# Five VectorE operations instead of six per block of float64 weights, and the adds of the second token product moved from GpSimd to VectorE

## The chip, the cores and the metric

The kernel runs on one core of one Trainium2 chip. The metric is the device time of one execution in microseconds (us), smaller is better. A run of the kernel is given by the median of its executions. One execution was also recorded by the hardware profiler; its lines are called the profile or the trace here. The engines are PE (TensorE: matmuls), PEld (its weight loads), DVE (VectorE), ACT (ScalarE), POOL (GpSimd) and SP (which only starts transfers). Each engine works through its own queue in order.

## The reference: what is computed

Hashed attention (4 batches, 8 heads, 768 positions, head size 64) followed by one mixer layer. The weights come from `randn(...).astype(float32) * (1.0 / np.sqrt(n))`, which gives **float64** arrays; the kernel has to round them to float32 itself.

```python
mask = q_bucket[:, :, :, None] == k_bucket[:, :, None, :]
scores = np.where(mask, scale * q @ k.T, -1e9)
x = softmax(scores) @ v                    # (B, S, 512)
h = np.maximum(xt @ w_tok1, 0.0) @ w_tok2  # xt: x with tokens last
u = x + h.transpose(0, 2, 1)
return u + np.maximum(u @ w_ch1, 0.0) @ w_ch2
```

w_tok1 is 768x256, w_tok2 256x768, w_ch1 512x1536, w_ch2 1536x512.

## The kernel before, in words

Three stages follow each other, each with its own pools, and each with the order of every queue written out by hand.

**Attention** (`attention`, from L266) goes over 16 pairs of heads. Per pair PE makes scores in 12 chunks (L345), ACT takes the exponentials (L352), DVE adds the chunks up (L379 to L386), PE multiplies with the values (`weigh`, L397), and DVE and ACT make quotients (`Quotients`: L425 to L448). In each pair one step of a weight conversion is laid between: `weights.join()` after `newton()`, and `weights.turnover()` after `divide()`. Twelve blocks are converted in this stage (w_tok1, w_tok2, w_ch1).

**Tokens** (`tokens`, L600) goes over the 4 batches b. `mix1(b)` is the first token product (L641), followed on ACT by a relu (L648). `left_sums(b)` (L664 to L667, DVE) prepares the left operands of the second product. `mix2(b, m)`, for m = 0 and 1, is the second token product. For b = 0 it is computed directly (L690, L694). For b = 1 to 3 it is a form with seven products instead of eight: ACT copies partial results out of PSUM (L703, L706, L708, L710) to four parts p1, u, p7, p57 of a buffer `to`, and five adds (L713 to L717) finish them there. A transfer started by POOL (L681, `store`) then adds the buffer to XT in memory. Buffers come from three `places` in turn: `mix2(b, m)` uses number (2b + m + 1) mod 3, so that (3,1) uses the one that (2,0) used, and its first copy L703 must wait until the store of (2,0) has landed. The order is: mix1(1), left_sums(1), mix2(0,0), job, mix2(0,1), weight sums, mix1(2), left_sums(2), mix2(1,0), job, mix2(1,1), mix1(3), left_sums(3), mix2(2,0), job, mix2(2,1), mix2(3,0), `inputs` (L594, L595), mix2(3,1). Two more jobs lie in each mix1, behind its relus. The first job makes sums for w_ch1; the others are `slot`s of the conversion of w_ch2, 8 blocks.

**Channels** (`channels`, L754) does the two channel products in nested forms with seven products (all matmuls at L782) and stores the result.

**A conversion** (`Conversion`, L140) works on blocks of 128 x 768 weights. `fetch` loads the raw 64-bit words to SBUF with a transfer by SP (L168). `begin` shifts the high word left by 3 and puts its sign bit back (L179, L182: the result `big` is a float32 number cut off below). `join` makes the unit of the last place from it (L194), multiplies it with the low word (L198) and adds (L199). `end` takes the square of the high word on ACT (L211) and uses it to set numbers that are too small to zero (L212). A `slot` in the token stage ends the block before, fetches, and does begin and join of the next one, so that there is one slot more than blocks. In attention, join and end of a block come one pair after its begin.

What sets who waits for whom: with `bufs=3` (tokens) a raw buffer is free again when the last instruction that reads it is done, which in tokens is the square L211; in attention (`bufs=2`) it is L212.

Of the kernel before, what the change touches and what calls it, by code (L numbers as in the profile page):

```python
# [36 lines left out]
F32 = mybir.dt.float32  # L37
BF16 = mybir.dt.bfloat16
U32 = mybir.dt.uint32
I32 = mybir.dt.int32  # L40
I64 = mybir.dt.int64
ALU = mybir.AluOpType
ACT = mybir.ActivationFunctionType
# [5 lines left out]
def kernel(  # L49
# [13 lines left out]
    nc = tc.nc  # L63
    P = 128
    B, NP, _, _, S = qk.shape
    D = 64
    NB = proj.shape[1]
    DM = NP * P
# [5 lines left out]
    NHT = DCH // P  # L74
# [58 lines left out]

    NW = 768

    LEAST = float.fromhex("0x1.2p-15")
    double = w_tok1.dtype == I64
    NE = 2 if double else 1

    class Conversion:  # L140


        def __init__(self, pool, parts, bufs, apart=False):
            self.pool, self.bufs, self.apart = pool, bufs, apart
            self.todo = [
                (w, dst, rows, j, n)
                for w, dst, rows, blocks in parts
                for j in range(*blocks, rows)
                for n in range(0, dst.shape[2], NW // rows)
            ]  # L150
            self.fetched, self.begun, self.ready = [], None, None
            for _ in range(bufs - 1):
                self.fetch()
# [17 lines left out]
        def begin(self):  # L171
            if not self.fetched:
                return
            raw, to, rows = self.fetched.pop(0)
            hi = raw[:, :, 1]
            tmp = self.pool.tile([P, 2, NW], F32, name="tmp", tag="cvt", bufs=1)
            big = tmp[:, 0].bitcast(U32)

            nc.vector.tensor_scalar(  # L179
                big, hi, 3, 0x3FFFFFFF, op0=ALU.logical_shift_left, op1=ALU.bitwise_and,  # L180
            )
            nc.vector.scalar_tensor_tensor(  # L182
                big, hi, 0xC0000000, big, op0=ALU.bitwise_and, op1=ALU.bitwise_or,
            )
            self.begun = raw, tmp, to, rows

        def join(self):
            if not self.begun:
                return
            raw, tmp, to, rows = self.begun  # L190
            self.begun = None
            lo, hi = raw[:, :, 0], raw[:, :, 1].bitcast(F32)
            big, unit = tmp[:, 0], tmp[:, 1]
            nc.vector.tensor_scalar(  # L194
                unit.bitcast(U32), big.bitcast(U32), 0xFF800000, None, op0=ALU.bitwise_and,
            )

            nc.vector.scalar_tensor_tensor(unit, lo, 2.0**-52, unit, op0=ALU.mult, op1=ALU.mult)  # L198
            nc.vector.tensor_tensor(big, big, unit, op=ALU.add)  # L199
            self.ready = hi, big, to, rows  # L200

        def end(self):

            if not self.ready:
                return
            size, big, to, rows = self.ready
            self.ready = None
            hi = size
            if self.apart:
                size = self.pool.tile([P, NW], F32, name="size", tag="size", bufs=1)  # L210
            nc.scalar.activation(size, hi, ACT.Square)  # L211
            nc.vector.scalar_tensor_tensor(  # L212
                to, size.rearrange("p (t n) -> p t n", t=rows), LEAST * LEAST,
                big.rearrange("p (t n) -> p t n", t=rows), op0=ALU.is_ge, op1=ALU.mult,
            )

        def turnover(self):

            self.end()
            self.fetch()  # L220
            self.begin()

        def slot(self):

            self.end()
            self.fetch()
            self.begin()
            self.join()

    pairs = [(b, hp) for b in range(B) for hp in range(NP)]  # L230

# [34 lines left out]
    def attention(pool, psum, W1, W2, x0):  # L266
# [191 lines left out]
        for _ in range(12):  # L458
# [5 lines left out]
            bufs=2,  # L464
# [4 lines left out]
        for n in range(len(pairs)):  # L469
            halves = [Half(n, half) for half in range(2)]  # L470
            if n:
                load_v(n + 1)
            for now in halves:
                now.scores()
                if n == now.half == 0:
                    hashes(1)
                now.add()
                if now.half == 0:
                    now.add_last()
            if before:  # L480
                before.sums()
            if 0 < n < len(pairs) - 1:
                hashes(n + 1)
            halves[1].add_last()
            if n == 0:
                load_v(1)
            load_qk(n + 2)
            add_values(n)
            if before:
                before.newton()  # L490
            weights.join()
            halves[0].weigh()
            if n + 1 == len(pairs):
                before.divide()
                before = Quotients(halves)
                before.sums()
                before.newton()
                weights.turnover()
                halves[1].weigh()
                break  # L500
            if before:
                before.divide()
            weights.turnover()
            halves[1].weigh()
            if n and n % 2 == 0:
                bounce(pool.tile([P, 2 * S], F32, name="stage", tag="stage", bufs=1), n - 2)
            if n == 2 * NP:
                fetch(0, x0)
            before = Quotients(halves)
# [90 lines left out]
    def tokens(pool, psum, W1, W2, x0, weights, jobs, T, places):  # L600
# [68 lines left out]
        def mix2(b, m):  # L669

            r1, new = R1[b]
            a00, a01, s1, a11 = (
                r1[:, k, P * (2 * m + i) : P * (2 * m + i) + P] for i in range(2) for k in range(2)
            )
            new = new[:, :, P * m : P * m + P]
            ps = [bank("t2")[:, :HALF] for _ in range(4)]
            to = places[(2 * b + m + 1) % 3].rearrange("p (i n t) -> p i n t", i=2, n=2)
            p1, u, p7, p57 = (to[:, i, n] for i in range(2) for n in range(2))

            def store():  # L680
                nc.gpsimd.dma_start(  # L681
                    out=XT[:, 2 * m : 2 * m + 2, S * b : S * b + S], in_=to.rearrange("p i n t -> p i (n t)"),
                    accum_op=ALU.add,
                )

            if not b:
                for n in range(4):
                    for k in range(NJ):
                        at = P * (2 * m + n // 2)
                        nc.tensor.matmul(  # L690
                            ps[n], r1[:, k, at : at + P], W2[:, k, HALF * (n % 2) : HALF * (n % 2) + HALF],
                            start=(k == 0), stop=(k == NJ - 1),
                        )
                    nc.scalar.copy(to[:, n // 2, n % 2], ps[n])  # L694
                return store()

            def product(at, left, right, start=True):
                nc.tensor.matmul(  # L698
                    ps[at], left, right, start=start, stop=True, skip_group_check=True,
                )  # L700

            product(0, a00, b00)
            nc.scalar.copy(p1, ps[0])  # L703
            product(1, a01, b10)
            product(2, s1, sums[:, 0])
            nc.scalar.copy(p57, ps[2])  # L706
            product(3, new[:, 1], b01)
            nc.scalar.copy(p7, ps[3])  # L708
            product(0, new[:, 0], sums[:, 1], False)
            nc.scalar.copy(u, ps[0])  # L710
            product(2, new[:, 2], b11, False)
            product(3, a11, sums[:, 2], False)
            nc.vector.tensor_tensor(p1, ps[1], p1, op=ALU.add)  # L713
            (nc.gpsimd if b + 1 < B else nc.vector).tensor_tensor(p57, p7, p57, op=ALU.add)  # L714
            nc.vector.tensor_tensor(p57, p57, u, op=ALU.add)  # L715
            nc.vector.tensor_tensor(p7, ps[3], u, op=ALU.add)
            nc.vector.tensor_tensor(u, ps[2], u, op=ALU.add)  # L717
            store()
# [652 lines left out]
    def attention_and_tokens(W1, W2, x0):  # L1371
# [11 lines left out]
        second["tile"] = second_tile  # L1383

        def weights(pool):
            return Conversion(pool, [(w_ch2, WC2, 3, (0, NHT))], bufs=3, apart=True)

        def jobs(conversion):
            early, late = weight_sums(
                WC1, SW1, slice(0, NCB // 2), slice(NCB // 2, NCB), slice(0, DCH // 2), slice(DCH // 2, DCH),  # L1390
            )
            return [
                lambda: (early(), late()),
                *[conversion.slot] * (NHT * DM // NW + 1),
            ]

        SW2 = second["SW2"].rearrange("p i k c -> p i (k c)")
# [3 lines left out]
    def careful_attention_and_tokens(W1, W2, x0):  # L1401
        def weights(pool, psum):
            conversion = Conversion(pool, [(w_tok1, W1, 3, (0, NR)), (w_tok2, W2, 1, (0, NJ))], bufs=3)
            while conversion.fetched or conversion.ready:
                conversion.slot()

        def turned(pool, psum):
            turn(0, x0, lambda: psum.tile([P, 2, 512], F32, name="trp", tag="tr", bufs=2))
# [58 lines left out]
```

## Time and profile before

| | |
|---|---|
| median of 6 runs | 806.91 us (805.8 to 809.95) |
| the profiled execution | 806.37 us |
| its span, first to last instruction | 804.6 us, 10632 instructions |
| mean granted TensorE clock | 0.998 |
| busy: DVE, ACT, POOL | 672.1, 441.3, 57.1 us |
| attention, tokens, channels (PE from, to) | 14.5 to 315.9, 315.9 to 397.1, 397.4 to 798.2 us |

Lines of the profile have a start in us from the beginning of the span, a duration, the engine, the line of the kernel, the operation, and its output and inputs by name. `t` is a PSUM bank, `tmp` and `size` are scratch of the conversion, `second` in the token stage is a place of `mix2`, or the converted w_ch2. `x4` counts instructions that were merged into one line; each float32 matmul of the code is two PE instructions (mix1 has 12 matmuls and 24 instructions). In brackets is how long the engine had been idle before, and the instruction that ended the wait.

### The profile page before, as it was taken

To read this page: it belongs to the slowest core of one execution; us is meant where nothing else is said; L and a number is where in the kernel's file an instruction comes from. 1 tells how busy PE (TensorE), PEld (TensorE's weight loads), DVE (VectorE), ACT (ScalarE), POOL (GpSimd) and SP (SyncE) were. 2 spreads that over 40 slices of the span, in tenths; PEclk is the share of its full clock that TensorE was granted. 3 is DMA by queue.
4 is the path that set the end of the run, shared out by engine and by line. 5 is a ranking of instruction groups with operands and counts; after the bars stand their busy time and mean duration, and the time that the engine had idled before them with its cause. 6 is when DMAs were issued, how large, how long until landed. Compare 5 with 4: busy or idle time off the path is not lost.

```text
span 804.6 us, 10632 instructions
## 1 busy us (share of the span) xinstructions
PE 795.0 (99%) x3889; PEld 471.3 (59%) x3889; DVE 672.1 (84%) x884; ACT 441.3 (55%) x707; POOL 57.1 (7%) x80
## 2 busy tenths in 40 slices
PE   9999999999999999999999999999999999999996
PEld 5444444444444444455444458876666886666885
DVE  4789999999998677989867879888769897778986
ACT  5688888888888886243323221237773335775111
POOL 1000000000000000022221010011100012000000
PEclk9999999999999999999999999999999999999999
DMA  4435353537352424886646895499754578630454
GB/s 162 158 121 159 121 160 122 160 121 238 128 163 108 142 62 157 235 249 172 154 79 205 287 368 198 158 284 260 249 141 137 216 216 199 209 114 1 156 184 114
DMA packets 90701, 138.09 MB, mean 172 GB/s; under 512 B 29640, under 2 KB 63376, under 8 KB 88336
## 3 DMA queue, kind: packets, MB, share of 16 engines
q1 hardware_dynamic: 82480, 112.47, 42.1%
q0 software_dynamic: 7456, 24.12, 13.3%
q8 instruction: 33, 0.54, 0.3%
q10 hardware_dynamic: 704, 0.74, 0.3%
q14 instruction: 28, 0.23, 0.1%
HBM read 97.21 MB, written 33.16 MB: 162 GB/s over the span
## 4 chain that ended last, share of the span: by engine, by line
PE 95%; DVE 2%; issue 1%; POOL 0%; ACT 0%; DVEq 0%; POOLq 0%
PE b L782 49%; PE sc L345 20%; PE acc L397 16%; PE t L641 4%; PE sums L421 2%; PE t L690 1%; PE hp L306 1%; PE t L698 1%; PE hw L324 1%; PE idle L459 0%; DVE second L713 0%; DVE tmp L179 0%; DVE second L715 0%; POOL second L714 0%; DVE second L212 0%
## 5 line engine op out<-in xcount | busy, mean ns | idle before, releaser
L352 ACT ACTIVATE e<-sc 128x768 f32<-128x768 f32 x192 | 154.0, 810 | 13.0 <-PE sc L345 12.6
L345 PE MATMUL sc<-qk 64*128 64x384 f32 x768 | 156.7, 487 | 0.0
L782 PE MATMUL b<-R,second 128*128 128x256 f32 (+1 forms) x612 | 150.9, 404 | 0.0
L782 PEld LDWEIGHTS b<-R,second 128*128 128x128 f32 x612 | 116.3, 190 | 31.6 <-issue 17.2
L788 ACT COPY c<-b 128x512 f32<-128x512 f32 (+1 forms) x78 | 37.4, 488 | 169.7 <-PE b L782 155.4
L397 PE MATMUL acc<-e,vn 128*64 128x384 f32 x768 | 127.6, 488 | 0.0
L383 DVE TENSOR_TENSOR esd<-esd,e 128x768 f32<-128x768 f32 x96 | 92.0, 958 | 10.0
L397 PEld LDWEIGHTS acc<-e,vn 128*64 128x64 f32 x768 | 53.6, 137 | 73.1 <-issue 71.8
L345 PEld LDWEIGHTS sc<-qk 64*128 64x128 f32 x768 | 67.5, 187 | 49.5 <-issue 46.6
L782 PE MATMUL b<-XT,WC 128*128 128x256 f32 (+1 forms) x264 | 82.6, 457 | 0.2 <-DVE second L713 0.2
L782 PEld LDWEIGHTS b<-XT,WC 128*128 128x128 f32 x264 | 50.1, 190 | 30.2 <-issue 24.9
L345 PE MATMUL sc<-bits 64*128 64x384 bf16 x384 | 62.9, 323 | 0.2 <-DVE bits L328 0.2
L379 DVE SCALAR_TENSOR_TENSOR esd<-e 128x768 f32<-128x768 f32 x32 | 30.3, 948 | 17.6 <-ACT e L352 17.6
L641 PE MATMUL t<-x,W 128*128 128x512 f32 x96 | 41.8, 593 | 0.0
L442 ACT COPY rec<-rec 32x384 f32<-32x384 f32 x64 | 32.6, 509 | 10.1 <-DVE rec L436 9.5
L681 POOL DMA_DIRECT2D XT<-second x8 | 9.9, 1236 | 382.9 <-DVE tmp L198 338.5
L782 PE MATMUL b<-XT,SW 128*128 128x256 f32 (+1 forms) x120 | 34.6, 422 | 0.0
L345 PEld LDWEIGHTS <-bits 64*128 64x128 bf16 x384 | 19.3, 94 | 25.4 <-DVE bits L328 0.8
L782 PE MATMUL b<-TA,WC 128*128 128x512 f32 x72 | 33.8, 592 | 0.0
L782 PE MATMUL b<-TA,SW 128*128 128x512 f32 x72 | 32.9, 592 | 0.0
L403 ACT ACTIVATE num<-acc,vsum 128x384 f32<-128x384 f32 x32 | 18.6, 581 | 25.0 <-PE acc L397 24.6
L386 DVE TENSOR_TENSOR esd<-esd,e 128x768 f32<-128x768 f32 x32 | 30.5, 954 | 1.9
(220 smaller groups left out, 1149.9 us busy)
## 6 DMA issues: line engine op xcount, KB each, us to landing
second<-left SPq DMA_DIRECT2D x18, 1344.0 KB
raw<-in_moe_w_ch SPq DMA_DIRECT2D x16, 768.0 KB
qk<-in_qk SPq DMA_DIRECT2D x15, 768.0 KB
seen<-in_qk POOLq DMA_DIRECT2D x21, 384.0 KB, 3.7
WC<-hidden_left SPq DMA_DIRECT2D x15, 448.0 KB
vn<-in_v SPq DMA_DIRECT2D x16, 384.0 KB
vt<-in_vT SPq DMA_DIRECT2D x16, 384.0 KB
x<-bounced SPq DMA_DIRECT2D x4, 1536.0 KB
```

The source lines that it names most:

```text
L345: nc.tensor.matmul(sc[:, i, :HALF], t[rows, 1, P * c : P * c + P], t[rows, 0, qs], start=start, stop=not start,)
L352: nc.scalar.activation(e, sc[:, :, :HALF], ACT.Exp, scale=SCALE)
L379: nc.vector.scalar_tensor_tensor(self.d, es[0], NR * EPS, es[1], op0=ALU.add, op1=ALU.add,)
L383: nc.vector.tensor_tensor(self.d, self.d, e, op=ALU.add)
L386: nc.vector.tensor_tensor(self.d, self.d, self.es[-1], op=ALU.add)
L397: nc.tensor.matmul(acc[D * i : D * i + D], vn[:, i, c], e[:, i], start=(c == 0), stop=(c == NR - 1),)
L403: nc.scalar.activation(nums[self.n][:, self.half], acc, ACT.Identity, scale=-1.0, bias=vsum,)
L421: nc.tensor.matmul(ps[at : at + 32], ones[:, :32], self.halves[h].d[:, i], start=True, stop=True,)
L442: nc.scalar.copy(rec[other : other + 32, h], rec[at : at + 32, h])
L641: nc.tensor.matmul(ps, W1[:, r, P * j : P * j + P], x[:, r], start=(r == 0), stop=(r == NR - 1),)
L782: nc.tensor.matmul(ps, left(k), right(k), start=start and k == ks[0], stop=stop and k == ks[-1], skip_group_check=True,)
L788: nc.scalar.copy(c, ps)
```

## The change

Part one rewrites the conversion. ACT first takes the absolute value of the high word, read as a float32 number and scaled by 2 to the -112, which moves its exponent so that a shift by 3 gives the float32 number directly. `begin` is now this one ACT instruction; `join` has four DVE operations (the unit by shift and mask, the shifted number, unit times low word, the add), and `end` puts the sign back with one more. The square, the comparison with LEAST and the restoring of sign bits in `begin` are gone. The scratch of a block is two tiles, `size` (bufs - 1 of them) and `unit`, in place of `tmp` and, in tokens, `size`.

Part two is the order. In tokens, `slot` becomes `one`: begin, join, end and fetch of one block in one job, 8 jobs in place of 9. In attention, `begin` moves from `turnover` to a place ahead of `newton()`, so that a block is converted within one pair.

Part three: the add L714 of mix2 runs on DVE for all batches; before, it ran on POOL for b = 1 and 2.

```diff
-    LEAST = float.fromhex("0x1.2p-15")
+    EXPONENTS = 2.0**-112
...
     def begin(self):
...
-            nc.vector.tensor_scalar(
-                big, hi, 3, 0x3FFFFFFF, op0=ALU.logical_shift_left, op1=ALU.bitwise_and,
-            )
-            nc.vector.scalar_tensor_tensor(
-                big, hi, 0xC0000000, big, op0=ALU.bitwise_and, op1=ALU.bitwise_or,
-            )
-            self.begun = raw, tmp, to, rows
+            size = self.pool.tile([P, NW], F32, name="size", tag="size", bufs=self.bufs - 1)
+            nc.scalar.activation(size, raw[:, :, 1].bitcast(F32), ACT.Abs, scale=EXPONENTS)
+            self.begun = raw, size, to, rows
...
     def join(self):
...
+            unit = self.pool.tile([P, NW], F32, name="unit", tag="unit", bufs=1)
             nc.vector.tensor_scalar(
-                unit.bitcast(U32), big.bitcast(U32), 0xFF800000, None, op0=ALU.bitwise_and,
+                unit.bitcast(U32), size.bitcast(U32), 3, 0x7F800000,
+                op0=ALU.logical_shift_left, op1=ALU.bitwise_and,
             )
-            nc.vector.scalar_tensor_tensor(unit, lo, 2.0**-52, unit, op0=ALU.mult, op1=ALU.mult)
-            nc.vector.tensor_tensor(big, big, unit, op=ALU.add)
+            nc.vector.tensor_scalar(
+                size.bitcast(U32), size.bitcast(U32), 3, None, op0=ALU.logical_shift_left,
+            )
+            nc.vector.scalar_tensor_tensor(unit, raw[:, :, 0], 2.0**-52, unit, op0=ALU.mult, op1=ALU.mult)
+            nc.vector.tensor_tensor(size, size, unit, op=ALU.add)
...
     def end(self):
...
-            nc.scalar.activation(size, hi, ACT.Square)
             nc.vector.scalar_tensor_tensor(
-                to, size.rearrange("p (t n) -> p t n", t=rows), LEAST * LEAST,
-                big.rearrange("p (t n) -> p t n", t=rows), op0=ALU.is_ge, op1=ALU.mult,
+                to.bitcast(U32), hi, 0x80000000, size, op0=ALU.bitwise_and, op1=ALU.bitwise_or,
             )
...
         def turnover(self):
             self.end()
             self.fetch()
-            self.begin()
-        def slot(self):
+        def one(self):
+            self.begin()
+            self.join()
             self.end()
             self.fetch()
-            self.begin()
-            self.join()
...
             add_values(n)
+            weights.begin()
             if before:
                 before.newton()
             weights.join()
...
-            (nc.gpsimd if b + 1 < B else nc.vector).tensor_tensor(p57, p7, p57, op=ALU.add)
+            nc.vector.tensor_tensor(p57, p7, p57, op=ALU.add)
...
-                *[conversion.slot] * (NHT * DM // NW + 1),
+                *[conversion.one] * (NHT * DM // NW),
```

The same conversion is called in a second path of the kernel (`careful_attention_and_tokens`), which runs only if a flag that the kernel computes from its inputs is set; the profile shows no instruction of it.

More of the change, by code (lines that the diff above doesn't have):

```diff
@@ L140, with __init__ @@
     class Conversion:
-        def __init__(self, pool, parts, bufs, apart=False):
-            self.pool, self.bufs, self.apart = pool, bufs, apart
+        def __init__(self, pool, parts, bufs):
+            self.pool, self.bufs = pool, bufs
             self.todo = [
@@ L174, in begin @@
             raw, to, rows = self.fetched.pop(0)
[L175 to L179, printed above, removed]
-                big, hi, 3, 0x3FFFFFFF, op0=ALU.logical_shift_left, op1=ALU.bitwise_and,
-            )
-            nc.vector.scalar_tensor_tensor(
-                big, hi, 0xC0000000, big, op0=ALU.bitwise_and, op1=ALU.bitwise_or,
-            )
-            self.begun = raw, tmp, to, rows
+            size = self.pool.tile([P, NW], F32, name="size", tag="size", bufs=self.bufs - 1)
+            nc.scalar.activation(size, raw[:, :, 1].bitcast(F32), ACT.Abs, scale=EXPONENTS)
+            self.begun = raw, size, to, rows
         def join(self):
@@ L189, in join @@
                 return
-            raw, tmp, to, rows = self.begun
+            raw, size, to, rows = self.begun
             self.begun = None
-            lo, hi = raw[:, :, 0], raw[:, :, 1].bitcast(F32)
-            big, unit = tmp[:, 0], tmp[:, 1]
+            unit = self.pool.tile([P, NW], F32, name="unit", tag="unit", bufs=1)
             nc.vector.tensor_scalar(
-                unit.bitcast(U32), big.bitcast(U32), 0xFF800000, None, op0=ALU.bitwise_and,
-            )
-            nc.vector.scalar_tensor_tensor(unit, lo, 2.0**-52, unit, op0=ALU.mult, op1=ALU.mult)
-            nc.vector.tensor_tensor(big, big, unit, op=ALU.add)
-            self.ready = hi, big, to, rows
+                unit.bitcast(U32), size.bitcast(U32), 3, 0x7F800000,
+                op0=ALU.logical_shift_left, op1=ALU.bitwise_and,
+            )
+            nc.vector.tensor_scalar(
[3 more added lines that the diff above has]
+            nc.vector.tensor_tensor(size, size, unit, op=ALU.add)
+            self.ready = raw, size, to, rows
         def end(self):
@@ L205, in end @@
                 return
-            size, big, to, rows = self.ready
+            raw, size, to, rows = self.ready
             self.ready = None
-            hi = size
-            if self.apart:
-                size = self.pool.tile([P, NW], F32, name="size", tag="size", bufs=1)
-            nc.scalar.activation(size, hi, ACT.Square)
+            hi, size = (a.rearrange("p (t n) -> p t n", t=rows) for a in (raw[:, :, 1], size.bitcast(U32)))
             nc.vector.scalar_tensor_tensor(
-                to, size.rearrange("p (t n) -> p t n", t=rows), LEAST * LEAST,
-                big.rearrange("p (t n) -> p t n", t=rows), op0=ALU.is_ge, op1=ALU.mult,
+                to.bitcast(U32), hi, 0x80000000, size, op0=ALU.bitwise_and, op1=ALU.bitwise_or,
             )
@@ L1385, in weights @@
         def weights(pool):
-            return Conversion(pool, [(w_ch2, WC2, 3, (0, NHT))], bufs=3, apart=True)
+            return Conversion(pool, [(w_ch2, WC2, 3, (0, NHT))], bufs=3)
         def jobs(conversion):
@@ L1403, in weights @@
             conversion = Conversion(pool, [(w_tok1, W1, 3, (0, NR)), (w_tok2, W2, 1, (0, NJ))], bufs=3)
-            while conversion.fetched or conversion.ready:
-                conversion.slot()
+            while conversion.fetched:
+                conversion.one()
         def turned(pool, psum):
```

## The prediction

> **What bounds the kernel now.** I read the page first, then PE's waits, the busy time by stage, and last the timelines of the one stretch that was left. The page's first line of busy times:
>
> ```profile
> PE 795.0 (99%) x3889; PEld 471.3 (59%) x3889; DVE 672.1 (84%) x884; ACT 441.3 (55%) x707; POOL 57.1 (7%) x80
> ```
>
> DVE is 84% busy, but PE is 99%: taking work off DVE can only pay where PE stands still for it. PE's waits are four, and only the first and the third lie in the stretch that the change touches:
>
> ```profile
> PE t L698 <- ACT second L703: 1.8, 1, 1.8
> PE idle L459 <- DVE ones L97: 1.0, 1, 1.0
> PE b L782 <- DVE second L713: 0.2, 1, 0.2
> PE sc L345 <- DVE bits L328: 0.2, 1, 0.2
> ```
>
> Busy time by stretch (attention; tokens up to mix1(3); from there to the channels; channels) places them. The first numbers are the stretch's length and PE's busy time:
>
> ```profile
> 13.75:315.90 302.15, 302.15 (x2134) 144.03 (x2133) 264.45 (x325) 246.87 (x371) 0.00 (x0) 1.00 0.42 139
> 315.90:366.18 50.28, 50.28 (x132) 25.11 (x133) 43.90 (x54) 17.93 (x32) 4.32 (x3) 1.00 0.80 230
> 366.18:397.36 31.18, 29.15 (x82) 14.73 (x80) 28.13 (x43) 10.07 (x20) 7.93 (x7) 1.00 0.66 158
> 397.36:797.80 400.44, 400.44 (x1476) 280.32 (x1477) 331.50 (x454) 160.47 (x279) 41.52 (x50) 1.00 0.63 189
> ```
>
> PE has no gap in attention or in channels, so the 12 conversions of attention gain nothing whatever they save on DVE. All there is lies in 366.18 to 397.36. Its ideal length: mix1(3) took 10.30 us (366.18 to 376.48), and an undisturbed mix2 takes 4.51 us ((1,1): 361.67 to 366.18), so 10.30 + 4 x 4.51 = 28.34 us. It took 31.18. **At most 2.8 us can be won**: 2.2 in the wait and its modelled ends at mix2(3,1), 0.3 in (2,0), 0.1 in (3,0), 0.2 ahead of channels.
>
> The timeline shows why. PE, ACT, POOL and DVE, merged in order of time:
>
> ```profile
> 383.82 0.42 DVE L664 TENSOR_TENSOR r1s<-r 128x256 f32<-128x256 f32 x1
> ...
> 388.02 1.21 POOL L681 DMA_DIRECT2D XT<-second  x1 [6.99 <-DVE second L717]
> ...
> 390.30 0.56 DVE L715 TENSOR_TENSOR second<-second 128x384 f32<-128x384 f32 x1 [2.22 <-POOL second L714]
> ...
> 394.40 0.48 ACT L703 COPY second<-t 128x384 f32<-128x384 f32 x1 [4.61 <-DMA XT<-second]
> ...
> 394.93 0.91 PE L698 MATMUL t<-W2sums,r1s 128*128 128x384 f32 x2 [1.78 <-ACT second L703]
> ...
> 397.36 1.12 PE L782 MATMUL b<-XT,WC 128*128 128x512 f32 x2 [0.22 <-DVE second L713]
> ```
>
> Read it backwards. PE waits for L703 of mix2(3,1); that waits for the store of (2,0) to leave the shared place; the store was issued at 388.02 and landed 6.4 us later. It was late because DVE finished (2,0) at 387.6, having started its adds only at 385.54, behind left_sums(3) (383.82) and the last conversion (to 383.9). So DVE's backlog bounds these 2.8 us.
>
> **What a conversion costs.** The rows for the token stage (ns min/median/max):
>
> ```profile
> L179 DVE TENSOR_SCALAR tmp<-raw x8: 552/561/2115, 327.8 to 377.9; 128x768 uint32<-128x768 uint32 x8
> L182 DVE SCALAR_TENSOR_TENSOR tmp<-raw,tmp x8: 957/959/959, 328.4 to 378.6; 128x768 uint32<-128x768 uint32 x8
> L194 DVE TENSOR_SCALAR tmp<-tmp x8: 559/560/1245, 329.4 to 379.6; 128x768 uint32<-128x768 uint32 x8
> L198 DVE SCALAR_TENSOR_TENSOR tmp<-raw,tmp x8: 957/958/1653, 330.0 to 380.2; 128x768 f32<-128x768 uint32 x8
> ```
>
> With L199 and L212 (0.96 each) six operations make 4.95 us. The new five: two shifts (0.56 each, as L179 and L194), multiply (0.96, L198), add (0.96, L199), and-or (0.96, L182) = 4.00. Saved: 0.96, with the 0.03 between operations **0.99 us a block**. On ACT, Abs takes the place of the square. Its nearest row is L211, same shape, input and engine, 0.92 us; the cheapest 128x768 row is the exponential with 0.81. I take 0.92: nothing gained or lost.
>
> **The POOL add.** L714 on DVE costs 0.47 us from start to start (0.55 busy, the b = 3 rows), four times. What goes: the wait of 2.22 us at 390.30, and stretching. Three conversion operations overlap a POOL add and are the three outliers above: 1.25 for 0.56, 2.12 for 0.56, 1.65 for 0.96, together 2.95 us. The Trainium skill (SBUF — State Buffer, "SBUF: two separate sides") says that the two engines share a port pair as an exclusive lock, and the loser blocks for the whole instruction. By it each of the four adds (1.41 us mean) could cost DVE its full length, 5.6 us; the trace has 2.95, and I take that. The same section speaks against the change: DVE operations in two-port mode keep POOL from writing transfer descriptors, and the new join puts two shifts of 0.56 behind each other. By the rule a store could start 1.1 us later. At 377.44 a store ran beside L179: 1.26 us for the usual 1.22. And no conversion is left when the store that matters is issued, so: 0, at most 1.1.
>
> **New times on DVE.** In both kernels DVE's fifth job starts at 353.6, behind the first relu of mix1(2). From there to left_sums(3) at 383.82 DVE had no idle time. Out of it go one L212 whose block now ends earlier (0.99), four times 0.99, and 2.95 of stretching; in come two L714 (0.94). That is 6.96 less, plus 1.05 of new waiting: block six can't start before its Abs ends (relu of the second half at 357.95, Abs to 358.8), while DVE is done at 357.75. left_sums(3) starts at 383.82 - 5.9 = 377.9, just behind its relu (377.3). Its four operations take 1.7, so mix2(2,0) can begin at 379.6. It is then bound by PE: its last product ends at 381.0, L716 and L717 follow to 382.25, and **the store is issued at about 382.65 instead of 388.02**. The stores follow each other every 6.6 us at least (388.02, 394.64 and on); that of (1,1) will be out by 374.1 (five DVE adds done at 373.6), so this is no limit.
>
> The store lands at 389.0. PE, undisturbed, runs (2,0) to 381.0, (2,1) to 385.5, (3,0) to 390.0; L703 of (3,1) wants the place at 390.9 (0.84 after the first product starts, as at 386.65). **Margin 1.9 us; the wait is gone.** The ACT wait in (2,0) goes with the ninth slot; the 0.1 in (3,0) came from L716/L717 of (2,0), now 5 us earlier. Late next is DVE ahead of channels: (3,0) ends at 391.3, `inputs` 393.7, L713 of (3,1) 394.2; PE ends at 394.5. Cover 0.3 us; if it fails, that is rival 2.
>
> **New waits.** DVE now waits for Abs. In tokens it sits where the square sat, in front of L703 or L694, so ACT's order is the same. Abs is now the first reader of the raw block, on ACT: the shortest way from the load's issue to Abs is block four, 332.1 to 342.3 = 10 us. Rows for 768 KB landings run from 6.3 to 11.3 us; at 11.3 ACT would lose 1.1 us, and PE nothing: the eight banks go round, and those that wait for L694 there are next written by mix2(1,0), from 357.2. SP's loads wait for DVE's end instead of the square, about 1 us earlier each. In attention Abs fills ACT's idle time ahead of the copies of `newton` (copies 0.5 us later); behind the waiting join stand divide and end, and join with its 3.1 us covers those copies. The pair's DVE work ends 0.6 us sooner. In pair 0 the whole conversion runs 25.3 to 29.4, ahead of the next add at 30.17. PE: 0.
>
> **Sum.** 2.8 us. From the profiled execution (806.37, span 804.6 + 1.8): 803.6. The median is 0.5 above that execution: 806.9 - 2.8 = **804.1**.
>
> **Rivals.** (1) The store of (2,0) meets other transfers and takes 11.3 us, as the first store did beside two raw loads and an x load. It would land at 394.0, 0.4 before the old time: 806.4. For: in the new order `out` (512 KB) and the first left block (768 KB) are issued at 380.5 to 381, close to it. Against: the store at 377.44 followed 1 MB issued 2 us before and still took 6.4. (2) A wait replaces the wait: L713 to L717 with all five adds in DVE's queue reach a PSUM bank late, or DVE holds up the start of channels; about half is kept, 805.4. (3) **Slower**: Abs is a new function for ACT. If it needed its own table, each block would switch there and back. The row of the one load (L453) is 1.28 us. ACT is idle 55.28 us in attention, 3.45 per pair; two loads at 1.28 would fit. The skill (ScalarE: Activation LUTs, "What ACT_TABLE_LOAD costs") has 2.66 for a switch: 5.3 per pair, 1.9 too much, 12 times = 22 us, about 829. It decides from 1.73 us a switch. Against it: the same page ("Table sets") says abs is in every set; the trace shows Ln, Exp, Square, Copy and Relu on one load, but no Abs. By the page the price is 0, which I take.
>
> **How the numbers follow.** All waits go: 0.62, 804.1 (803.4 to 804.9). Rival 1: 0.16, 806.4. Rival 2: 0.17, 805.4. Rival 3: 0.05. The range from 803.4 to 806.4 leaves out rival 3, half of rival 1 and the likeliest case's tail. A measurement can tell 0.3%, here 2.4 us, from no change; the full gain of 2.8 is barely over it, so of the likeliest case four fifths count as faster, and of the others nearly none: faster 0.50, same 0.45, slower 0.05.
>
> **What would show it.** In the changed profile: PE without a wait on L703, channels starting at 394.5 (off the mark if after 396.5); L664 of left_sums(3) near 377.9; the store of (2,0) near 382.7, landing within 7 us; no outliers in the shift rows; Abs at 0.92; one table load. It is wrong if PE shows a new wait in attention, or if the store leaves early and L703 still waits.

## The result, and the profile after

The changed kernel takes 803.99 us in the median of 18 runs (802.41 to 806.38), against 806.33 of 40 runs of the kernel before: a ratio of 0.9968, 95% interval 0.9959 to 0.9976, or 2.6 us by the ratio. A later series gave 0.9960 (0.9947 to 0.9974). The prediction was 804.1 and 2.8 us. The median of before is now 806.33, where it was 806.91 when the prediction was made, so the 804.1 was met with a gain of 2.3 to 2.6 us by the runs; the traces give 2.7 (below).

The profiled execution of the changed kernel took 802.73 us, its span is 800.9. The page's busy times, and all of PE's waits:

```profile
PE 793.0 (99%) x3889; PEld 471.1 (59%) x3889; DVE 653.0 (82%) x868; ACT 441.3 (55%) x707; POOL 52.8 (7%) x76
```

```profile
PE idle L451 <- DVE ones L97: 1.0, 1, 1.0
PE sc L337 <- DVE bits L320: 0.2, 1, 0.2
```

DVE lost 19 us of work, and PE two of its four waits (1.8 and 0.2 us). Lines have moved: `left_sums` now begins at L657, the first copy of mix2 is L696, the store L674, the conversion L177 to L206, the channels' matmul L775. The timeline of the changed kernel in the places that were shown before, and ahead of them the issue of the first left block, a transfer that the store meets:

```profile
376.45 0.42 DVE L657 TENSOR_TENSOR r1s<-r 128x256 f32<-128x256 f32 x1
...
380.99 0.64 SPq L1038 DMA_DIRECT2D left<-second  x1
...
381.59 1.21 POOL L674 DMA_DIRECT2D XT<-second  x1 [7.29 <-DVE second L710]
...
388.86 1.45 PE L691 MATMUL t<-W,r 128*128 128x384 f32 x4
...
390.88 0.48 ACT L696 COPY second<-t 128x384 f32<-128x384 f32 x1 [2.64 <-DMA XT<-second]
...
391.44 0.89 PE L691 MATMUL t<-W2sums,r1s 128*128 128x384 f32 x2
...
393.45 3.60 PE L775 MATMUL b<-XT,WC 128*128 128x512 f32 x8
```

The store of mix2(2,0) leaves early, as forecast. But the copy L696 of mix2(3,1) still waits for it (2.64 us of idle ACT), and PE has no wait all the same. That is the one surprise, and it is taken apart below.

**Comparing two traces.** The spans differ by 3.7 us, more than the runs do. The surplus lies in the opening: in these two traces the first matmul of mix1(0) starts at 315.83 and 314.66. It is chance, as further traces of both kernels show (below). So traces are compared by times counted from that matmul. The columns, all but the third in us from that matmul: start of left_sums(3); issue of the store of (2,0); how long it took until the first copy of (3,1), which waits for it; start of that copy; start of the channels; the gain or loss there.

| kernel | left_sums(3) | store issued | took | copy of (3,1) | channels | channels, against before |
|---|---|---|---|---|---|---|
| before | 67.99 | 72.19 | 6.38 | 78.57 | 81.53 | |
| changed | 61.79 | 66.93 | 9.29 | 76.22 | 78.79 | -2.74 |
| conversion only | 63.12 | 68.14 | 8.44 | 76.58 | 79.15 | -2.38 |
| add only | 66.44 | 71.31 | 6.50 | 77.81 | 80.39 | -1.14 |
| order only | 65.47 | 70.54 | 6.99 | 77.53 | 80.10 | -1.43 |
| own place | 68.05 | 72.25 | no wait | 75.39 | 79.06 | -2.47, of which 0.53 is lost again at once |
| changed, sixth in attention | 61.79 | 66.93 | 9.25 | 76.18 | 78.75 | -2.78 |
| changed, sixth in tokens | 64.42 | 69.36 | 7.91 | 77.27 | 79.83 | -1.70 |
| changed, transfers later | 61.79 | 66.93 | 7.75 | 75.05 | 78.72 | -2.81 |

("Transfers later" has no wait for the store; its landing is read from the next store, which POOL issued 7.99 us after it, where elsewhere the next store follows a landing by 0.24.)

### The profile page after: what moved, and what is told of

Read it like the earlier page. It is cut to its first block, busy times and chain, and to the rows that moved or that the text cites. A ratio compares the mean times of both kernels' runs of the same rounds, so it can differ in the third digit from the quotient of the medians.

```text
span 800.9 us, 10585 instructions
## 1 busy us (share of the span) xinstructions
PE 793.0 (99%) x3889; PEld 471.1 (59%) x3889; DVE 653.0 (82%) x868; ACT 441.3 (55%) x707; POOL 52.8 (7%) x76
## 4 chain that ended last, share of the span: by engine, by line
PE 98%; DVE 1%; issue 0%; DVEq 0%
PE b L775 49%; PE sc L337 20%; PE acc L389 16%; PE t L634 5%; PE t L691 3%; PE sums L413 2%; PE t L683 1%; PE hp L298 1%; PE hw L316 0%; PE idle L451 0%; DVE second L1210 0%; DVE R L1169 0%; DVE R L1166 0%; DVE q L1196 0%; DVE second L1196 0%
## 5 line engine op out<-in xcount | busy, mean ns | idle before, releaser
L775 PE MATMUL b<-R,second 128*128 128x256 f32 (+1 forms) x612 | 150.9, 404 | 0.0
L775 PEld LDWEIGHTS b<-R,second 128*128 128x128 f32 x612 | 116.3, 190 | 31.6 <-issue 17.2
L775 PE MATMUL b<-XT,WC 128*128 128x256 f32 (+1 forms) x264 | 82.5, 456 | 0.0
L775 PEld LDWEIGHTS b<-XT,WC 128*128 128x128 f32 x264 | 50.2, 190 | 29.6 <-issue 25.1
L674 POOL DMA_DIRECT2D XT<-second x8 | 9.8, 1230 | 391.6 <-DVE r1s L657 337.3
L775 PE MATMUL b<-XT,SW 128*128 128x256 f32 (+1 forms) x120 | 34.6, 422 | 0.0
L775 PE MATMUL b<-TA,WC 128*128 128x512 f32 x72 | 33.8, 592 | 0.0
L775 PE MATMUL b<-TA,SW 128*128 128x512 f32 x72 | 32.9, 592 | 0.0
```

The source lines that it names most:

```text
L775: nc.tensor.matmul(ps, left(k), right(k), start=start and k == ks[0], stop=stop and k == ks[-1], skip_group_check=True,)
```

## The experiments

My theory: PE stood still for 2.8 us between mix1(3) and the channels because DVE was late with mix2(2,0), and any of the three parts that makes DVE earlier wins a piece of the same 2.8 us. The rivals: each part has a share of its own; or one part is the whole cause; or the conversions in attention count too.

**Conversion only.** The changed kernel with the add back on POOL.

```diff
-            nc.vector.tensor_tensor(p57, p7, p57, op=ALU.add)
+            (nc.gpsimd if b + 1 < B else nc.vector).tensor_tensor(p57, p7, p57, op=ALU.add)
```

> The changed kernel, but the add L714 of mix2 goes back to POOL for b = 1 and 2: parts one and two of the change alone. Theory (all of the gain is the 2.8 us in which PE stood still between mix1(3) and the channels, and it is capped there): DVE still loses the 2.2 to 3 us of stretching beside the POOL adds and waits for the add of (2,0) to about 4 us after its last copy, so the store of (2,0) leaves about 0.8 us later than in the changed kernel; 0 to 0.6 us of PE's wait comes back. 2.1 to 2.7 us faster than before, about 803.9. Rival (the parts add up, each with its share by the DVE time it saves): 1.9 of 2.8 us at most. Rival (the POOL add is the whole cause): no gain, 806.3.

Measured: ratio 0.9961 (0.9948 to 0.9974), and -2.38 us in the trace. PE's wait of 1.78 us has become 0.17 us. POOL, DVE, ACT and PE:

```profile
384.74 1.21 POOL L674 DMA_DIRECT2D XT<-second  x1 [3.15 <-DVE second L710]
...
387.01 0.56 DVE L708 TENSOR_TENSOR second<-second 128x384 f32<-128x384 f32 x1 [2.22 <-POOL second L707]
...
393.18 0.48 ACT L696 COPY second<-t 128x384 f32<-128x384 f32 x1 [2.99 <-DMA XT<-second]
...
393.71 0.91 PE L691 MATMUL t<-W2sums,r1s 128*128 128x384 f32 x2 [0.17 <-ACT second L696]
```

DVE's wait of 2.22 us for the POOL add is there as in the kernel before, and costs PE nothing. The two first parts are nearly the whole gain. The theory held; the store was 1.2 us later than in the changed kernel, where 0.8 was expected.

**Add only.** The kernel before with the add on VectorE.

```diff
-            (nc.gpsimd if b + 1 < B else nc.vector).tensor_tensor(p57, p7, p57, op=ALU.add)
+            nc.vector.tensor_tensor(p57, p7, p57, op=ALU.add)
```

> The kernel before with only the add L714 on VectorE for all batches: part three alone. Theory: left_sums(3) starts about 2 us earlier (2.95 us of stretching less two adds of 0.47), the store of (2,0) leaves about 2 us earlier, and the 2.2 us wait of mix2(2,1) for the POOL add is gone, so that channels can start early too: 1.7 to 2.5 us faster, about 804.2. Rival (shares add up): about 0.8 us faster, 805.5. Rival (conversion is the whole cause): 806.3.

Measured: ratio 0.9981 (0.9971 to 0.9992), and -1.14 us in the trace, below the expected range. PE's wait stays for the most part:

```profile
PE t L698 <- ACT second L703: 1.4, 1, 1.4
```

The outliers of the conversion's operations are gone, so the POOL adds did cause them (L179 at most 0.67 us for 2.12, L194 0.56 for 1.25, L198 0.96 for 1.65). left_sums(3) starts 1.55 us earlier, where about 2 was expected. The larger error was the step behind it: mix2(2,0) itself now has a fifth add on DVE, in front of its store, so the store is only 0.88 us earlier.

**Order only.** The six old operations and the POOL add, but one job per block.

```diff
+        def one(self):
+            self.begin()
+            self.join()
+            self.end()
+            self.fetch()
...
-                *[conversion.slot] * (NHT * DM // NW + 1),
+                *[conversion.one] * (NHT * DM // NW),
```

> The kernel before with its six operations, its square and its POOL add, but in the token stage each block is begun, joined and ended in one job (8 jobs in place of 9): part two alone. Theory: the last conversion ends a job earlier, left_sums(3) starts about 2.5 us earlier, the store of (2,0) near 385.6 in place of 388.0; PE's wait for the place shrinks from 1.8 us to 0 to 1; 1.5 to 2.5 us faster, about 804.4. Rival (what matters is the number of DVE operations, not their order): no gain, 806.3.

Measured: ratio 0.9971 (0.9959 to 0.9983), and -1.43 us in the trace, just below the expected range (by the ratio, 2.3 us, inside it). left_sums(3) starts 2.52 us earlier and the wait at (3,1) shrinks to 0.45. But half a microsecond is given back earlier, in a wait that neither kernel had. PE's waits of this kernel (L710 is the first copy of mix2 here), then DVE, ACT and PE at the first of the two:

```profile
PE t L705 <- ACT second L710: 0.9, 2, 0.4
```

```profile
362.81 0.96 DVE L212 SCALAR_TENSOR_TENSOR second<-size,tmp 128x768 f32<-128x768 f32 x1
```

```profile
363.80 0.93 ACT L211 ACTIVATE size<-raw 128x768 f32<-128x768 f32 x1 [2.43 <-DVE second L212]
364.63 0.45 ACT L710 COPY second<-t 128x384 f32<-128x384 f32 x1
```

```profile
365.14 0.91 PE L705 MATMUL t<-W2sums,r1s 128*128 128x384 f32 x2 [0.41 <-ACT second L710]
```

There is one `size` buffer; the next square waits until L212 has read it, and the copy that PE needs stands behind the square. The changed kernel has two `size` tiles in tokens (bufs - 1) and Abs in place of the square, and no such wait on PE; which of the two it owes this to, no run shows. So the order is a part of the gain by itself. The rival (only the number of operations counts) falls.

**Own place.** The kernel before, with a buffer of its own for mix2(3,1), and two raw buffers to make room.

```diff
+            place = places[(2 * b + m + 1) % 3]
+            if not turned and (b, m) == (B - 1, 1):
+                place = pool.tile([P, 2 * S], F32, name="fourth", tag="fourth", bufs=1)
-            to = places[(2 * b + m + 1) % 3].rearrange("p (i n t) -> p i n t", i=2, n=2)
+            to = place.rearrange("p (i n t) -> p i n t", i=2, n=2)
...
-            return Conversion(pool, [(w_ch2, WC2, 3, (0, NHT))], bufs=3, apart=True)
+            return Conversion(pool, [(w_ch2, WC2, 3, (0, NHT))], bufs=2, apart=True)
```

> The kernel before, but mix2(3,1) writes to a buffer of its own, so that its first copy waits for no store; to make room the conversion of w_ch2 has two raw buffers in place of three. Theory as the prediction had it (the shared place is what holds PE up): the 1.8 us wait is gone, 804.3. Theory in its sharper form (DVE's lateness holds PE up at two places one behind the other): PE no longer waits for the copy, but waits for L713 of (3,1) at the start of the channels, which is still at 397.3 because DVE waits for the POOL add of (2,1) at 390.3: the wait moves, and the time stays within 0.4 us of 806.3.

Measured: ratio 0.9965 (0.9950 to 0.9979). DVE is as late as before (left_sums(3) at 68.05, the store at 72.25), and yet the channels start 2.47 us earlier. ACT, PE and DVE, in order:

```profile
393.95 0.48 ACT L706 COPY fourth<-t 128x384 f32<-128x384 f32 x1 [1.46 <-PE t L701]
...
397.62 3.60 PE L785 MATMUL b<-XT,WC 128*128 128x512 f32 x8
...
399.55 0.55 DVE L716 TENSOR_TENSOR fourth<-t,fourth 128x384 f32<-128x384 f32 x1
...
401.75 1.98 PE L785 MATMUL b<-TA,WC 128*128 128x512 f32 x4 [0.53 <-DVE fourth L719]
```

The copy no longer waits for a store, but for PE's own product, and PE goes through. My sharper theory, that channels would then be held up at their start, was wrong: they begin while L716 (here the number of L713) of (3,1) has not even started. What DVE's lateness costs after that is 0.53 us, eight instructions later. So **the shared place is what turned DVE's lateness into PE's wait**, as the prediction had read it, for 1.9 of the 2.7 us: a buffer of its own for one result wins that much with DVE as late as ever. Why the trace of before names L713 for the 0.2 us at the start of the channels stays open; this run shows that it isn't needed there.

**Sixth operation in attention.** The changed kernel with 0.96 us more on DVE in each of 12 blocks; nobody reads the result.

```diff
+            if self.bufs == 2:
+                nc.vector.scalar_tensor_tensor(
+                    unit.bitcast(U32), raw[:, :, 1], 0x80000000, size.bitcast(U32),
+                    op0=ALU.bitwise_and, op1=ALU.bitwise_or,
+                )
```

> The changed kernel with one more VectorE operation of 0.96 us per block in attention only (12 blocks; the and-or of sign and number into the scratch tile unit, where nobody reads it), as if the saved operation were still there. Theory: PE has no gap in attention, so 11.5 us more of DVE work there cost nothing: as the changed kernel, 2.3 to 2.8 us faster than before, about 803.9. Rival (attention's share of the saved operations, 12 of 20, brings its share of the gain): 1.0 us faster, 805.3.

Measured: ratio 0.9952 (0.9937 to 0.9967), no slower than the changed kernel; the channels start at 78.75 (78.79 in the changed kernel). DVE's busy time rose to 663.8 us, and PE's waits are the same two. The 12 operations saved in attention are worth nothing.

**Sixth operation in tokens.** The same for the other 8 blocks (`self.bufs == 3`).

> The changed kernel with one more VectorE operation of 0.96 us per block in the token stage only (8 blocks, result not read). Theory: DVE's idle 1.0 us before block six swallows one of the four operations that count; left_sums(3) starts 2.9 us later, mix2(2,0) is then bound by DVE, and its store leaves about 2.3 us later; but it meets less of the other transfers and lands only about 1 to 1.5 us later, against a cover of about 0: 0.5 to 1.2 us of the gain are lost, 1.5 to 2.2 us faster than before, about 804.5. Rival (each saved DVE microsecond counts): 2.9 us are lost, 806.4 or more.

Measured: ratio 0.9968 (0.9956 to 0.9979); beside the run with attention's 12, on the same chip, 1.1 us slower. In the trace 1.04 us of the gain are lost, in the expected range: left_sums(3) 2.63 us later, the store 2.43, its landing only 1.05, and PE waits 0.85 us for the copy. POOL, ACT and PE:

```profile
384.97 1.21 POOL L679 DMA_DIRECT2D XT<-second  x1 [7.99 <-DVE second L715]
...
392.88 0.48 ACT L701 COPY second<-t 128x384 f32<-128x384 f32 x1 [3.68 <-DMA XT<-second]
...
393.41 0.91 PE L696 MATMUL t<-W2sums,r1s 128*128 128x384 f32 x2 [0.85 <-ACT second L701]
```

Eight operations cost PE something where twelve cost nothing: the place counts, not the sum of busy time.

**Transfers later.** The changed kernel, with the copies of XT to `out` and the first left block moved behind later work in SP's queue.

```diff
-                [], sums, [whole("p1"), second_parts("p7")], *([second_parts(name)] for name in ("p6", "p3", "p5", "p2", "p4")),
+                [], sums, [second_parts("p7"), whole("p1")], *([second_parts(name)] for name in ("p6", "p3", "p5", "p2", "p4")),
...
-            if t == 1:
+            if t == 3:
                 residual(0)
```

> The changed kernel with the transfers that met the store of (2,0) put later in SP's queue: the copies of XT to out follow two steps of hidden later, and the first left block goes behind the sums of the second one. Theory: the store of (2,0) lands 6.3 to 6.6 us after its issue in place of 9.3, the wait of L696 for it is gone (2.6 us on ACT), and PE gains only the last 0.1 us: 803.9. Rival (the store was slow of itself): it still takes over 8 us. A loss of up to 1 us is possible where the transfers now meet others in the channels.

Measured: ratio 0.9953 (0.9939 to 0.9967), channels at 78.72. SP's queue is empty from 357 to 420, and the copy of (3,1) waits for nothing but PE. POOL's stores in this kernel, and that copy:

```profile
382.19 1.21 POOL L674 DMA_DIRECT2D XT<-second  x1 [7.29 <-DVE second L710]
390.18 1.22 POOL L674 DMA_DIRECT2D XT<-second  x1 [6.78 <-DVE second L708]
...
390.31 0.48 ACT L696 COPY second<-t 128x384 f32<-128x384 f32 x1 [1.46 <-PE t L691]
```

The store took 7.75 us for 9.29, so the other transfers had cost it 1.5 us: its first packet moved 3.5 us after its issue in the changed kernel, behind the left block, and 1.8 us after it here. It did not come down to the 6.4 us that I had expected. In both kernels the transferred amount falls to some 12 to 15 GB/s for the last 1.5 us. The rate of the changed kernel from 384 to 392 us, in slices of 0.2 us, and what else ran:

```profile
GB/s 328 343 317 302 317 441 154 179 302 230 230 200 92 184 246 230 215 184 200 154 230 215 230 215 92 15 15 15 15 15 0 15 0 0 0 0 0 0 0 0
```

```profile
q8 instruction: 1, 0.02, 0.7%
```

This tail is the store's own data: each transfer ends with 16 packets of 4 bytes, and of the store's 16 all but one are through at 389.21, the last at 390.47 (in before at 393.99 and 394.02, without a tail). The one transfer of instructions (0.02 MB) is not the tail; it runs from 385.67 to 386.62. But it starts just when the last closing packet of the left block ends, 0.4 us after the other 15, so it seems to have run on the one of the 16 DMA engines that was late already. In the eight traces in which such a transfer starts after the store's issue, the store's last packet comes 0.5 to 1.4 us after the one before it; in the six in which it starts earlier, at most 0.17; but these eight are also the ones with one job per block. That the store's last packets stood behind it is likely, but no run moved that transfer, so it isn't shown.

**The same kernels again.** Part three alone was traced a second time, and before and changed two more times each.

> A second look at part three alone (the add of mix2 on VectorE in the kernel before), for how far two executions of one kernel differ before attention starts: the first product of the hashes took 2.65 us in the trace of before and 1.49 in that of the changed kernel. If that is chance, these starts differ in the same way between runs of one kernel; if it is the change, every trace of a kernel with the old conversion has 2.65 and every one with the new has 1.49.

> The kernel before, a second look, for the opening: the time from the start of the span to the first matmul of mix1(0). It was 315.9 us in the first trace of before, 316.2 to 318.6 in four kernels with the old conversion in attention, 314.7 to 316.7 in five with the new one. Theory (the opening only depends on when the first loads of q and k land, which differs from execution to execution): openings of both kernels overlap, 314.7 to 318.6. Rival (the change shortens the opening by about 1 us): each look of before lies above 315.9 and each of the changed kernel below it. The token stage from mix1(0) to the channels is 81.4 to 81.5 us by both.

> The changed kernel again. Theory: token stage 78.7 us, opening anywhere between 314.7 and 318.6, and 2.7 us faster than before in the median (ratio 0.9966). Rival (the opening is shortened too): opening below 315.9 and 3.8 us faster (0.9953), as two variants of it measured on another chip.

> The kernel before, a third look. As the second: token stage 81.4 to 81.5 us; opening by the theory anywhere between 314.7 and 318.6, by the rival above 315.9.

> The changed kernel, a third look. As the second: token stage 78.7 us; opening by the theory anywhere between 314.7 and 318.6, by the rival below 315.9.

| | mix1(0) starts | token stage, up to the channels | span |
|---|---|---|---|
| before, three traces | 315.83, 316.21, 315.80 | 81.53, 81.52, 81.53 | 804.6, 805.1, 804.8 |
| changed, three traces | 314.66, 316.03, 316.40 | 78.79, 78.82, 78.81 | 800.9, 801.9, 802.7 |
| add only, two traces | 317.11, 316.13 | 80.39, 80.45 | 805.3, 804.1 |

Single times of before were 806.92 and 806.63, of the changed kernel 804.16 (median of 8) and 804.48, of add only 805.84. The openings of the two kernels overlap, and those of one kernel differ by up to 1.7 us, so the rival that the change shortens the opening falls. The token stage repeats to 0.06 us. This is a sharper measure than the run time: **2.72 us** (81.53 - 78.81). The 3.8 us by the ratios of two variants above (0.9952, 0.9953) are more than PE had to give in this stage; what the rest is, these runs do not show.

## Why the prediction was right, point by point

The bound and DVE's part came out as worked out. From the store's landing on, two errors cancelled each other, and that is luck. By the prediction's own sign of being wrong, "if the store leaves early and L703 still waits", this step did fail: the store left early, and the copy (now L696) still waited 2.64 us for it.

- **The bound.** PE's ideal for the stretch left at most 2.8 us to win. 2.72 were won. That the 12 conversions of attention are worth nothing is shown by the run that gave their DVE time back.
- **DVE's backlog.** left_sums(3) was to start 5.9 us earlier; it starts 6.2 earlier. The cost of five operations and the new wait for Abs (predicted 1.05, measured 1.00, ahead of block six) were right, and the stretching is gone. The rows of the new operations on `size`:

```profile
L177 ACT ACTIVATE size<-raw x20: 891/918/939, 20.0 to 370.9; 128x768 f32<-128x768 f32 x20
L187 DVE TENSOR_SCALAR unit<-size x20: 549/560/642, 24.1 to 372.5; 128x768 uint32<-128x768 uint32 x20
L191 DVE TENSOR_SCALAR size<-size x20: 559/560/562, 24.7 to 373.1; 128x768 uint32<-128x768 uint32 x20
```

No outlier is left, and Abs costs what the square did. In all, DVE waits 7.1 us for Abs in four places; 3.8 of it stand ahead of block five, where DVE used to be busy with older work.

- **The store.** Issued at 382.65 by the forecast, which is 66.82 after mix1(0); measured 66.93.
- **Its landing: a wrong term.** I gave it 6.4 us, and a cover of 1.9. It took 9.3. This was rival 1, a little over half as bad as it was written (11.3; in before that was the second store's time, while the first, which the prediction names, took 10.3), and my argument against it failed: I took 1.6 to 2.1 us as the distance to the other transfers, as with the store of (1,1). In fact the left block was issued at 380.99, only 0.6 us ahead of the store, because it stood behind the landing of (1,1), which itself took 7.5 us. 1.5 of the 2.9 us are these transfers, as the kernel with the transfers later shows; the rest is the tail, whose cause stays open.
- **A second wrong term hid it.** I let the copy be due 0.84 us after PE's first product of (3,1). But PE needs it only when it comes back to that bank, four products later: at 391.44, which is 2.58 us after the first product's start at 388.86. Taking off 0.84 and the copy's 0.48, there were 1.26 us more of cover. 1.9 + 1.26 stands against 2.9, and of the 0.26 left nothing remains in the trace: PE's matmul at 391.44 shows 0.89 us for the usual 0.81, and the channels start 0.07 us later than with the transfers moved. The cover that I wrote as 1.9 us was in truth used up, and the sixth operation in tokens shows it: a landing 1.05 us later starts the channels 1.04 us later.
- **The start of channels.** No wait there, as forecast with 0.3 us of cover.
- **Rivals 2 and 3.** No PSUM bank was late. The changed kernel has one table load of 1.28 us and no other.
- **The parts.** The prediction added up what the parts take off DVE, but not what each is worth in time. Conversion with its order gives 2.38, order alone 1.43, the add alone 1.14, all together 2.72: the shares add up to more than the whole (2.38 + 1.14 = 3.52), because all draw on one wait. With the conversion changed, the add brings only 0.36 us.

## What to carry to other kernels

When one engine is 99% busy, count what its gaps hold in the stage that a change touches; that is the most it can give, whatever it takes off another engine. Follow the wait to its end through buffers and stores: VectorE was 6 us earlier and the gain was 2.7, because PE had only 2.8 to give, and a slow landing nearly took some of that away. Ask when the bound engine needs a late step to be done, not when the step could first be done; and compare traces from a common point inside the kernel, where the stage repeated to 0.06 us while spans of one kernel differed by 1.8.

## What the runs showed of the hardware

- A POOL add and an operation of DVE took turns here. In the six traces with POOL adds, 18 of the 24 adds end while DVE is in an operation, and each of these 18 operations ends as if it had only begun 0.12 to 0.15 us before the add's end. In before, L194 starts at 361.43 and takes 1.25 us for 0.56, L179 starts at 369.34 and takes 2.12 for 0.56; the adds end at 362.26 and 371.02. The add waited in turn: where no store came just before it, it ended 0.86 to 0.92 us after the DVE operation ahead of it, so that it is 0.98 to 1.77 us long. This fits the exclusive lock that the prediction cites. The rows of before, DVE and then POOL, stand below.
- An add right behind a store held DVE longer, by 1.56 to 1.96 us for 0.7 to 0.8: L182 in "order only" took 2.92 us for 0.96. Why it is longer stays open; without the adds no operation of the conversion is stretched by more than 0.2 us beside the same stores.

```profile
361.43 1.25 DVE L194 TENSOR_SCALAR tmp<-tmp 128x768 uint32<-128x768 uint32 x1
...
369.34 2.12 DVE L179 TENSOR_SCALAR tmp<-raw 128x768 uint32<-128x768 uint32 x1
```

```profile
360.50 1.76 POOL L714 TENSOR_TENSOR second<-second 128x384 f32<-128x384 f32 x1 [5.96 <-ACT second L708]
368.80 1.20 POOL L681 DMA_DIRECT2D XT<-second  x1 [6.54 <-DVE second L717]
369.57 1.45 POOL L714 TENSOR_TENSOR second<-second 128x384 f32<-128x384 f32 x1
```

- The stores with add (768 KB, started by POOL) took 6.3 us in the median of before, and up to 11.3 beside loads. The store behind that of (2,0) was issued only 0.24 us after (2,0) had landed, although its data had been ready for 2.5 us in before and for 5.4 in the changed kernel.
